# Padding two groups of SBUF tiles in a fused attention and token/channel mixer to multiples of 256 bytes

## The chip, the cores and the metric

The kernel runs on one core of one Trainium2 chip. The metric is the device time of one execution in microseconds. Three runs of the kernel before gave 799.47, 801.26 and 802.11 us; their median, 801.26 us, is the time that the change is measured against. All matrix work is in fp32 or in fp32r, a form of fp32 that TensorE takes in one pass; where full precision is wanted an fp32 value is held as a high and a low fp32r part.

## The reference, cut to what matters

```python
# B, H, S, D = 8, 8, 576, 64; attention inside chunks of 64 positions
scores = q_c @ k_c.T / sqrt(D);  attn = softmax(scores)
x = (attn @ v_c) as (B, S, 512)
h  = relu(x.T @ w_tok1) @ w_tok2          # tokens: 576 -> 256 -> 576
u  = x + h.T
h2 = relu(u @ w_ch1) @ w_ch2              # channels: 512 -> 1536 -> 512
return u + h2
```

## The kernel before, in words

All weights stay in SBUF as a high and a low part (tiles `kept_*`; for the channel matrices 24 tiles of 4096 bytes in each partition, made one after another from raw words while batch 0 is computed). A product of two split operands is three matmuls, `THREE`: high weight by high data, low weight by high data, high weight by low data. On TensorE the `kept_c` slice of 128 columns is the stationary operand (the "weights", loaded by LDWEIGHTS while the matmul before it streams) and the data tile is the moving operand of 512, 448 or 288 columns.

The work falls into three stages.

1. **The start** (about the first 54 us): nine attention tiles' loads, weight conversion, five attention tiles of batch 0, whose `v` tiles have 65 columns a head (a column of ones gives the row sums) and are allocated with `VPAD` columns, and batch 0's token mixing. Its result, split in high and low parts for two halves of 288 positions and four groups of 128 channels, is the one tile `both`.
2. **Batch 0's channel mixing** (to about 152 us): `ch1` (L584) and `ch2` (L626) run over 12 slices `f` with the pieces of `both`, or the hidden tiles `gh`, `gl`, as moving operands of 288 columns. Beside it ACT and DVE convert the rest of the weights and attention of batch 1 runs.
3. **Eight blocks of 512 positions** (the last one 448), here numbered 0 to 7, to the end. In each, for each of 12 slices `f`: 12 matmuls at L584 (four channel groups by `THREE`; moving operands `uh`, twice each, and `ul`, once each, four tiles of both), ACT and DVE write the hidden slice as `gh` and `gl`, and 12 matmuls at L626 (moving operands `gh` eight times, `gl` four times). At some `f` an attention step (L325 and L337, 64 small matmuls in the trace) is put in between. At the end of a block stand the token matmuls of a later batch (L491, L562).

TensorE's order is written by hand; DMAs are all issued from SP's queue in program order; ACT, DVE and POOL are ordered by a planner, which also places every SBUF tile at an address, for the time that it lives.

**Where the tiles lie.** In the program of the kernel before, the planner stacked the tiles by size. At the bottom lies `both` (address 1152, 18432 bytes a partition), above it `g1` (19584), the first weights, `xt` and `kept_t2`; from 68736 to 183424 a stack of 28 slots of 4096 bytes (the kept channel weights and `qk`); above it three slots of 2176 bytes for `v` tiles of the start (183424, 185600, 187776); and from 189952 to 228864 a stack of 19 slots of 2048 bytes. Tiles of 2048 bytes (`gh`, `gl`, `uh`, `ul`, `xh`, `xl`, `rh`, `rl` and others) lie in that upper stack, and also below, wherever a larger tile has died. Taken modulo 256, every data tile of 512 bytes or more below 183424 starts at 128 (with one exception, a `ul` of the last block); 2176 is 128 more than a multiple of 256; and every slot of 2048 bytes from 189952 up starts at 0. The channel weights all start at 128. Thus a moving operand "agrees" with its weights modulo 256 if it starts at 128. The tiles at the places that the prediction speaks of:

| groups of 12 matmuls | moving operands' addresses | of 12, agreeing |
|---|---|---|
| L584, block 0 | uh 194048 212480 218624 226816, ul 185600 198144 202240 214528 | 0 |
| L584, block 1 | uh 28800 51328 57472 183424, ul 33408 187776 208384 220672 | 10 |
| L584, block 2 | uh 43136 45184 47232 214528, ul 30848 35456 202240 226816 | 8 |
| L584, block 3 | uh 51328 55424 183424 212480, ul 21632 33408 53376 216576 | 9 |
| L584, block 4 | uh 30848 43136 45184 194048, ul 35456 196096 202240 218624 | 7 |
| L584, block 5 | uh 26240 55424 57472 212480, ul 51328 208384 210432 216576 | 7 |
| L584, block 6 | uh 1152 41600 177280 181376, ul 3200 35456 53376 179328 | 12 |
| L626, most slices | gh 222720 or, at every other slice, 37504; gl 224768 or 206336 | 0 or 8 |
| L626, block 6 at 675.8 us | gh and gl both at multiples of 256 | 0 |
| L626, block 6 at 681.4 us | gh at 128, gl at 0 | 8 |
| L626, block 6 at 692.4 us | gh 222720, gl 17536 | 4 |
| L626, block 6 at 697.8 us | gh 39552, gl 7296 | 12 |

In block 7, of 448 columns, the L626 groups at 745.4 and 760.1 us have 12 agreeing, the L584 groups 9, other L626 groups 0 or 8. The pieces of `both` are 1152 bytes apart, so every other one agrees.

Of the kernel before, what the change touches and what calls it, by code (L numbers as in the profile page):

```python
# [13 lines left out]
F32R = mybir.dt.float32r  # L14
# [4 lines left out]
P = 128  # L19
B, H, S, D = 8, 8, 576, 64  # L20
CH = 64
BK = 32
# [3 lines left out]
NDT = DM // P  # L26
# [3 lines left out]
HALF = S // 2  # L30
# [1 line left out]
QK = 2 * NHP * P  # L32
DV = D + 1
VW = 2 * NHP * DV
VPAD = -(-VW // BK) * BK
REBIAS = 2.0 ** -112
MOST = float.fromhex("0x1.dffcp-96")
THREE = ((0, 0), (1, 0), (0, 1))
# [28 lines left out]
def attention_mixer_kernel(ctx, tc, qk_in, vo_in, v_in, w1_in, w2_in, wc1_in, wc2_in, out):  # L67
# [22 lines left out]
    pool = ctx.enter_context(tc.tile_pool(name="pool", bufs=2))  # L90
# [39 lines left out]
    for key, src, lo, n in reversed(plan):  # L130
        name = "raw_" + "_".join(map(str, key))
# [128 lines left out]
    def load_v(i):  # L260
        if i < NTILE:
            v = pool.tile([P, VPAD], F32, tag="v1" if i > 4 else "v0", name="v", bufs=2 if i > 4 else 5)
            v = v[:, :VW].rearrange("p (a b c) -> p a b c", a=2, c=DV)
# [427 lines left out]
    r = [pool.tile([P, DM], F32, tag="gr", name="r", bufs=8) for _ in range(NT1)]  # L691
    nc.scalar.activation(out=r[0], in_=sums[0], func=AF.Relu)
    nc.vector.tensor_scalar_max(out=r[1], in0=sums[1], scalar1=0.0)
    both = pool.tile([P, 2, 2, NDT, HALF], F32R, tag="both", name="both", bufs=1)
    us = [[[both[:, n, w, m] for m in range(NDT)] for w in range(2)] for n in range(2)]
    low = None
    for m in range(NDT):
        convert(END_FILL[2 + m])
# [204 lines left out]
```

## Time and profile before

| | before |
|---|---|
| median of 3 runs | 801.26 us (799.47 to 802.11) |
| profiled execution, its own time | 799.71 us |
| span of the profiled execution | 797.9 us |
| TensorE busy | 783.7 us (98%) |
| weight loads (beside the matmuls) | 653.6 us (82%) |
| VectorE / ScalarE / GpSimd busy | 348.7 / 237.7 / 108.1 us |
| mean granted TensorE clock | 0.993 |

The page's first part gives busy time by engine, its fourth the chain of work that ended last. A matmul's record is longer than its turn, because the next one starts before it has drained; what a matmul costs in a row of matmuls is therefore read from start to start, or from the length of a merged piece of the chain divided by its count.

### The profile page before, as it was taken

The page shows a single profiled execution, that of the slowest core. Times are in us where ns is not written, and L with a number is a line of the kernel's source. Part 1 is how long each engine was busy: PE and PEld are TensorE (multiplying, and loading weights), DVE is VectorE, ACT ScalarE, POOL GpSimd, SP SyncE. Part 2 cuts the span into 40 slices and gives each one's busy share as a digit, 9 for nine tenths or more (in the row PEclk, how much of TensorE's full clock was granted, in tenths as well). Part 3 has the DMA queues.
Part 4 walks back from the last instruction along what each step waited for, and adds up shares of the span by engine and source line. Part 5 has one row for each costly group of instructions (what it writes and reads, how often), then busy time and mean ns, then how long its engine had stood idle before and what let it go on. Part 6 is the DMA issues. An engine that isn't in the chain of part 4 may idle for free.

```text
span 797.9 us, 14108 instructions
## 1 busy us (share of the span) xinstructions
PE 783.7 (98%) x5857; PEld 653.6 (82%) x5857; DVE 348.7 (44%) x627; ACT 237.7 (30%) x418; POOL 108.1 (14%) x94
## 2 busy tenths in 40 slices
PE   7899999999999999999999999999999999999998
PEld 4589998887888888888888788888887788888997
DVE  5788756644344442543444334535343314114112
ACT  6899733322231221222322222222312211111110
POOL 0000011310012010401041004100130104003300
PEclk7999999999999999999999999999999999999999
DMA  9935334344413540343323430435134201000101
GB/s 355 407 118 201 129 95 136 100 139 138 146 32 123 162 133 14 118 162 132 113 67 126 143 97 37 161 129 160 37 115 131 80 1 53 0 1 14 40 0 47
DMA packets 66415, 87.60 MB, mean 110 GB/s; under 512 B 7792, under 2 KB 41328, under 8 KB 66352
## 3 DMA queue, kind: packets, MB, share of 16 engines
q1 hardware_dynamic: 66352, 86.71, 32.3%
q8 instruction: 46, 0.75, 0.4%
q14 instruction: 17, 0.14, 0.1%
HBM read 59.81 MB, written 25.95 MB: 107 GB/s over the span
## 4 chain that ended last, share of the span: by engine, by line
PE 87%; DVE 4%; DMA 4%; ACT 3%; issue 1%; SPq 1%; DVEq 0%; ACTq 0%
PE acc L626 35%; PE ps_c L584 33%; PE ps_t L562 6%; PE ps_t L491 6%; PE ps_sv L325 2%; DMA raw_c<-in_wc 2%; PE ps_sv L337 2%; PE ps_t L534 1%; DMA v<-in_vo 1%; ACT low L174 1%; PE ps_t L528 1%; ACT wtop L164 1%; DVE wtop L184 1%; DVE o L634 1%; SPq L359 1%
## 5 line engine op out<-in xcount | busy, mean ns | idle before, releaser
L626 PE MATMUL acc<-gh,kept_c 128*128 128x512 f32 (+2 forms) x960 | 275.4, 375 | 1.2 <-ACT gh L606 0.7
L584 PE MATMUL ps_c<-uh,kept_c 128*128 128x512 f32 (+1 forms) x768 | 236.8, 389 | 0.0
L596 DVE SCALAR_TENSOR_TENSOR gl<-ps_c,gh 128x512 fp32r<-128x512 f32 (+2 forms) x108 | 70.9, 656 | 322.6 <-ACT gh L595 322.6
L626 PEld LDWEIGHTS acc<-gh,kept_c 128*128 128x128 f32 x960 | 170.8, 188 | 32.1 <-ACT gh L606 1.2
L626 PE MATMUL acc<-gl,kept_c 128*128 128x512 f32 (+2 forms) x480 | 172.2, 372 | 0.0
L584 PEld LDWEIGHTS ps_c<-uh,kept_c 128*128 128x128 f32 x768 | 144.1, 188 | 30.7
L595 ACT ACTIVATE gh<-ps_c 128x512 fp32r<-128x512 f32 (+2 forms) x108 | 61.6, 570 | 298.2 <-PE ps_c L584 298.2
L584 PE MATMUL ps_c<-ul,kept_c 128*128 128x512 f32 (+1 forms) x384 | 149.5, 389 | 0.1
L626 PEld LDWEIGHTS acc<-gl,kept_c 128*128 128x128 f32 x480 | 88.1, 188 | 15.5
L434 POOL TENSOR_TENSOR xl<-x,xh 128x512 fp32r<-128x512 f32 x28 | 36.7, 1312 | 362.4 <-ACT xh L433 318.1
L584 PEld LDWEIGHTS ps_c<-ul,kept_c 128*128 128x128 f32 x384 | 72.1, 188 | 15.6 <-DVE ul L574 0.5
L574 POOL TENSOR_TENSOR ul<-u,uh 128x512 fp32r<-128x512 f32 (+1 forms) x16 | 20.8, 1305 | 259.1 <-ACT uh L573 247.2
L562 PE MATMUL ps_t<-kept_t,rh 128*128 128x448 f32 (+7 forms) x224 | 48.5, 311 | 0.0
L584 PE MATMUL ps_c<-both,kept_c 128*128 128x288 f32 x288 | 45.1, 302 | 0.1
L376 ACT COPY pt<-pf 128x512 f32<-128x512 f32 x31 | 19.2, 620 | 80.1 <-DMA pf<-far 80.1
L305 ACT ACTIVATE pr<-pr 128x512 f32<-128x512 f32 x36 | 22.7, 629 | 63.2 <-DVE pr L301 63.2
L584 PEld LDWEIGHTS ps_c<-both,kept_c 128*128 128x128 f32 x288 | 40.1, 188 | 1.3 <-DVE gl L596 0.2
L562 PEld LDWEIGHTS ps_t<-kept_t,rh 128*128 128x128 f32 x224 | 37.5, 189 | 1.7
L636 POOL TENSOR_TENSOR o<-o,ul 128x512 f32<-128x512 f32 x28 | 38.5, 1406 | 1.5 <-DVE o L634 1.5
L568 DVE TENSOR_TENSOR u<-ps_t,xt 128x512 f32<-128x512 f32 (+1 forms) x32 | 21.8, 681 | 35.1 <-PE ps_t L562 33.2
L573 ACT CAST uh<-u 128x512 fp32r<-128x512 f32 (+1 forms) x32 | 19.5, 614 | 53.0 <-DVE u L568 53.0
L491 PE MATMUL ps_t<-xh,kept_t 128*128 128x512 f32 x112 | 34.9, 393 | 0.0
(87 smaller groups left out, 703.2 us busy)
## 6 DMA issues: line engine op xcount, KB each, us to landing
qk<-in_qk SPq DMA_DIRECT2D x36, 512.0 KB, 3.9
far<-blocks SPq DMA_DIRECT2D x63, 256.0 KB, 2.1
raw_c<-in_wc SPq DMA_DIRECT2D x24, 512.0 KB, 9.1
pf<-far SPq DMA_DIRECT2D x124, 64.0 KB, 1.9
out<-o SPq DMA_DIRECT2D x28, 256.0 KB, 2.0
v<-in_v SPq DMA_DIRECT2D x27, 256.0 KB, 4.1
xt<-far SPq DMA_DIRECT2D x100, 64.0 KB, 1.9
v<-in_vo SPq DMA_DIRECT2D x9, 260.0 KB, 8.0
```

The lines of the kernel that those rows point to most:

```text
L305: nc.scalar.activation(out=pr, in_=pr, func=AF.Exp, scale=1.0 / float(D) ** 0.5)
L434: nc.gpsimd.tensor_tensor(out=xl, in0=t["x"], in1=xh.bitcast(F32), op=ALU.subtract)
L491: nc.tensor.matmul(ps, lhsT=lhsT, rhs=rhs, start=(n == 0 and q == 0), stop=(n == len(mt) - 1 and q == len(terms) - 1),)
L562: nc.tensor.matmul(ps[:, at:at + n], lhsT=lhsT[:, cols], rhs=rhs, start=(q == 0), stop=(q == len(terms) - 1),)
L568: nc.vector.tensor_tensor(out=u.rearrange("p (i c) -> p i c", c=BK), in0=ps[:, :width].rearrange("p (i c) -> p i c", c=BK), in1=block_x(k) ...
L573: nc.scalar.copy(out=uh[m], in_=u)
L574: (nc.vector if m in UL_ON_VECTOR else nc.gpsimd).tensor_tensor(out=ul[m], in0=u, in1=uh[m].bitcast(F32), op=ALU.subtract)
L584: nc.tensor.matmul(ps[:, :width], lhsT=weights["c1", f][:, wi, k * P:(k + 1) * P], rhs=u[ui][k], start=(k == 0 and q == 0), stop=(k == NDT ...
L595: nc.scalar.activation(out=gh, in_=ps[:, :width], func=AF.Relu)
L596: nc.vector.scalar_tensor_tensor(out=gl, in0=ps[:, :width], scalar=0.0, in1=gh.bitcast(F32), op0=ALU.max, op1=ALU.subtract)
L626: nc.tensor.matmul(accs[e], lhsT=weights["c2", f][:, wi, e * P:(e + 1) * P], rhs=g[gi], start=(f == 0 and q == 0), stop=(f == NFC - 1 and ...
L636: nc.gpsimd.tensor_tensor(out=o, in0=o, in1=u[1][e].bitcast(F32), op=ALU.add)
```

## The change

`VPAD`, the allocated width of the 65-column `v` tiles, is rounded up to 256 elements instead of 32: the tile takes 640 columns (2560 bytes) in place of 544 (2176 bytes). The last dimension of `both` grows from 288 to 320 columns (1280 bytes in place of 1152; the tile takes 20480 bytes), of which the first 288 are used. What is loaded, computed and written is the same, and so is the order in which it is written down.

```diff
-VPAD = -(-VW // BK) * BK
+VPAD = -(-VW // (8 * BK)) * 8 * BK
...
-    both = pool.tile([P, 2, 2, NDT, HALF], F32R, tag="both", name="both", bufs=1)
-    us = [[[both[:, n, w, m] for m in range(NDT)] for w in range(2)] for n in range(2)]
+    both = pool.tile([P, 2, 2, NDT, HALF + BK], F32R, tag="both", name="both", bufs=1)
+    us = [[[both[:, n, w, m, :HALF] for m in range(NDT)] for w in range(2)] for n in range(2)]
```

## Rows read from the trace of the kernel before

**Rows 1.** The page, parts 1 and 4: busy time by engine; the chain by engine.
```profile
PE 783.7 (98%) x5857; PEld 653.6 (82%) x5857; DVE 348.7 (44%) x627; ACT 237.7 (30%) x418; POOL 108.1 (14%) x94
PE 87%; DVE 4%; DMA 4%; ACT 3%; issue 1%; SPq 1%; DVEq 0%; ACTq 0%
```
**Rows 2.** Busy time by stretch: PE, weight loads, DVE, ACT, POOL, clock, DMA, GB/s.
```profile
0.00:54.00 54.00, 45.61 (x491) 31.42 (x492) 38.82 (x87) 42.17 (x75) 0.91 (x10) 0.91 0.85 325
54.00:152.00 98.00, 95.85 (x888) 89.82 (x888) 69.70 (x137) 59.89 (x119) 10.69 (x10) 1.00 0.39 125
...
570.00:660.00 90.00, 90.00 (x627) 74.35 (x626) 31.80 (x52) 18.22 (x30) 14.49 (x11) 1.00 0.22 72
660.00:735.00 75.00, 75.00 (x338) 62.41 (x337) 18.50 (x28) 10.70 (x19) 9.69 (x8) 1.00 0.04 15
```
**Rows 3.** Groups by line and shape: busy us, mean ns | idle before.
```profile
L626 PE MATMUL acc<-gh,kept_c 128*128 128x512 f32 x672 | 212.7, 397 | 0.0
L584 PE MATMUL ps_c<-uh,kept_c 128*128 128x512 f32 x672 | 209.5, 393 | 0.0
...
L626 PE MATMUL acc<-gl,kept_c 128*128 128x512 f32 x336 | 132.3, 394 | 0.0
L584 PE MATMUL ps_c<-ul,kept_c 128*128 128x512 f32 x336 | 132.0, 393 | 0.1
```
**Rows 4.** Chain in order of time, block 6 (no attention): start us, us, what.
```profile
675.83 2.79 PE acc L626 x12
...
681.36 2.75 PE acc L626 x12
684.10 2.72 PE ps_c L584 x12
...
692.35 2.75 PE acc L626 x12
...
697.84 2.72 PE acc L626 x12
```
**Rows 5.** The same, first two slices of L584 in blocks 1 to 6.
```profile
239.70 5.47 PE ps_c L584 x24
...
324.69 5.55 PE ps_c L584 x24
...
410.44 5.51 PE ps_c L584 x24
...
494.26 5.56 PE ps_c L584 x24
...
579.90 5.57 PE ps_c L584 x24
...
664.92 5.44 PE ps_c L584 x24
```
**Rows 6.** The same, blocks 0 and 1, with attention steps.
```profile
177.16 2.79 PE acc L626 x12
179.95 2.80 PE ps_c L584 x12
...
183.84 2.98 PE acc L626 x12
...
247.96 2.76 PE ps_c L584 x12
```
**Rows 7.** The same, block 7 of 448 columns.
```profile
742.97 2.43 PE ps_c L584 x12
745.40 2.47 PE acc L626 x12
...
750.31 2.45 PE acc L626 x12
```
**Rows 8.** The same, token matmuls at the end of block 5.
```profile
646.00 6.51 PE ps_t L491 x28
```
**Rows 9.** The chain from 60 to 112 us, shares by line.
```profile
by line: ACT low L174 11.5%; DMA raw_c<-in_wc 9.1%; DVE wtop L184 8.5%; ACT wtop L164 8.4%; issue 8.4%; DMA far<-blocks 7.7%; SPq L359 7.0%; DVE kept_c L231 6.8%; ACT low L165 4.4%; DVE wtop L178 4.2%; DVE blocks L348 3.1%; ACT kept_c L225 
```
**Rows 10.** Waits, whole span, then PE's from 152 us: us, times, longest us.
```profile
ACT pt L376 <- DMA pf<-far: 80.1, 30, 5.2
...
PEld ps_c L584 <- DVE ul L574: 0.5, 1, 0.5
```
**Rows 11.** DMA issues: count, KB each, median us from issue to landing.
```profile
v<-in_vo SPq DMA_DIRECT2D x9, 260.0 KB, 8.0
```

## The prediction, made before the change was run

> **What bounds the kernel now.** I read the page first: TensorE is busy for 98% of the span and carries 87% of the chain that ended last [rows 1]. Then the stretches: in the first 54 us ACT, DVE and DMA are as full as PE; from 54 to 152 us PE stands still for 2 of 98 us with DVE at 70 of them; from 570 to 660 us, one block with attention, PE is busy for all of it, the others for a third or less, and from 660 to 735 us, where there is no attention, it is the same with almost no DMA [rows 2]. So from 152 us on the kernel is a row of matmuls, and what a matmul takes from start to start is the time. The groups of 512 columns are 672 + 672 with high parts and 336 + 336 with low parts, 2016 matmuls in 168 groups of 12 [rows 3].
>
> The chain in order of time has these groups as pieces. In block 6, without attention, a piece of L626 takes 2.79, 2.75 or 2.72 us, with the same shapes and the same lines [rows 4]. What differs is where the moving operands lie, which the table of places gives: 2.79 with none of the 12 agreeing with the weights modulo 256, 2.75 with 8 and also with 4, 2.72 with 12. L584 shows the same over the blocks: a block's first two slices, 24 matmuls, take 5.44 us with 12 of 12 agreeing, 5.47 with 10, 5.51 with 9, 5.55 with 8, 5.56 and 5.57 with 7 [rows 5], and 2.80 for 12 with none [rows 6]. That is one order without an exception, over tiles in many places. I take it that a matmul whose moving operand lies 128 off from the weights being loaded beside it takes some 6 ns longer: (2.79 - 2.72) / 12.
>
> **The change, part by part.**
>
> *The v tiles.* No instruction is added or removed. The nine loads bring 260 KB each as before [rows 11]; the added columns are neither loaded nor read, so the start pays nothing for them, and the same holds for `both`. What changes is the stack of tiles: if the planner stacks by size as now, `both` and the 4096-byte tiles end at 183424 + 2048 = 185472, three slots of 2560 bytes end at 193152, and both are 128 modulo 256. The upper stack then starts at 128 instead of 0, and every `gh`, `gl`, `uh`, `ul`, `xh` and `xl` agrees with its weights wherever it lies. The order of the matmuls is written by hand, so only places and the waits for a place can change.
>
> What this is worth, by blocks 0 to 6. L584 goes to 2.72 a group: from 2.80 in block 0 [rows 6], and from half of the 24-matmul pieces in the others [rows 5]: 2.735 (later 2.76 [rows 6], which I take), 2.775, 2.755, 2.78, 2.785, 2.72. The gains are 0.08 + 0.04 + 0.055 + 0.035 + 0.06 + 0.065 + 0 = 0.335 us a slice, times 12 slices: 4.0 us. L626 goes from 2.79 or 2.75 to 2.72 [rows 4]; beside attention a group with 8 agreeing takes 2.79 as well [rows 6]. I take 72 groups of blocks 0 to 5 at a gain of 0.07, less about ten that run at 2.75 now and gain 0.03: 4.6 us; block 6 alternates, 12 groups at 0.04: 0.5 us. Together 9.1 us.
>
> The groups right after an attention step take 2.98 [rows 6], 0.19 more than their neighbours. The trace has none of these with 12 agreeing. Their extra may stay (I take that: the small matmuls before them have other operands) or go too, five to a block in six blocks, 30 x 0.1 = 3 us more at most if half of it goes; or the attention may take the gain away, which is a rival below.
>
> The token matmuls, L491: 28 in 6.51 us, 232 ns each [rows 8], against 2.72 / 12 = 227. Seven such pieces, 196 matmuls, about 1 us if all agree; some do now, so 0.8.
>
> The last block, 448 columns: here it is the other way round. The fully agreeing group takes 2.47 us, a group of 9 agreeing 2.43, one with none 2.45 [rows 7]. 24 groups at about +0.025 are 0.6 us lost.
>
> *The pieces of* `both`. They move to a spacing of 1280 bytes, so all agree instead of every other one. They are used in batch 0's stage alone. There the chain runs through conversions on ACT and DVE, DMAs and SP's queue, and no PE line has a place among the first dozen [rows 9]: a few ns a matmul are covered by waits for those. If that cover were gone the gain is at most the 2 us that PE now stands still for plus what the matmuls shrink; I take 0, and 0.5 us either way for the range.
>
> *Memory.* The upper stack has room for 17 slots of 2048 bytes instead of 19, (228864 - 193152) / 2048 = 17.4. The 4096-byte stack moves up by the 2048 bytes of `both`, and since `both` dies at about 152 us, one slot more is free below from then on. I take no new wait: in the main stage PE's longest wait for another engine is 0.5 us, once [rows 10].
>
> Sum: 4.0 + 5.1 + 0.8 - 0.6 = 9.3 us faster. Against its own execution, 799.7 us with a span of 797.9, that is 790.4; the median is 1.55 us above that execution, so 801.3 - 9.3 = 792.0 us.
>
> **The rivals.**
>
> *Attention keeps the groups late.* In block 1 the same L584 tiles take 2.735 a group at the block's start and 2.76 right after a slow L626 group [rows 5, 6]; and with 8 agreeing L626 takes 2.75 in block 6 but 2.79 in block 0 [rows 4, 6]. A group that starts late stays late. If each attention step sets that lateness afresh and agreement doesn't cure it, groups in blocks 0 to 5 settle near 2.76 in place of 2.72: 144 x 0.04 = 5.8 us of the gain are gone, and it comes to 801.3 - 3.5 = 797.8 us. Against it: in block 6 a 2.72 follows directly on a 2.75 [rows 4].
>
> *The planner doesn't stack as now.* It places tiles by their lives, and a sliver of 128 bytes or another count of `v` slots leaves some at 0. With half of the tiles agreeing about half is left: 796.7 us.
>
> *The places are not the cause.* The tiles at 0 are nearly all those of the upper stack, so the difference could come with the region, or with what runs when those tiles are in use. Then nothing changes: 801.3 us. Against it: 183424 and 187776 count as agreeing in blocks 1 and 3 and fit the order [rows 5], and in block 6 neighbours with one load differ [rows 4].
> [...]
>
> *Slower: a place comes free later.* With two slots fewer in the upper stack, the `pf` tile of an attention step (the transposed probabilities, fetched by DMA for ACT's copy at L376) may get a slot whose last reader ends later. SP's queue is in order, so the fetch and all loads behind it wait, ACT's copy is late, and TensorE stands at L337, since its order is fixed. ACT waits for that DMA in 30 steps already, 80.1 us in all [rows 10], covered by the matmuls of a slice or more. If the cover is used up, 31 steps at the 0.5 us of the longest PE wait [rows 10] cost 15.5 us: 801.3 - 9.3 + 15.5 = 807.5 us. It decides from (9.3 + 2.4) / 31 = 0.38 us a step. The third of idle time on the other engines [rows 2] speaks against it.
>
> **How the numbers follow.** About 0.3%, 2.4 us, is what a measurement of this kernel can tell from no change, so faster means under 798.9 us, slower over 803.7. Forecast 792.0 us: 0.65. Attention keeps groups late, 797.8: 0.13, of which 0.09 is under 798.9. Half the tiles, 796.7: 0.08, of which 0.06 under. No cause, 801.3: 0.07. Slower, 807.5: 0.07. Faster 0.65 + 0.09 + 0.06 = 0.80; same 0.04 + 0.02 + 0.07 = 0.13; slower 0.07. The range goes down to 788.5 (the 3 us after attention steps and 0.5 for batch 0) and up to 799.5, which takes in the first two rivals with the spread of 1.5 us between runs, and leaves out 0.07 + 0.07 and some ends.
>
> **What would show it.** In the changed profile the 24-matmul pieces of L584 should be 5.44 in every block, L626's pieces 2.72 in block 6 without alternation, the L491 piece 6.35, the block 7 pieces 2.47, and the stage up to 152 us as long as now. L584 pieces at 2.76 beside attention show the first rival; a mix of 2.72 and 2.79 the second; unchanged pieces with all places at 128 the third; new idle time of PE ahead of L337 the last. The prediction fails if agreement isn't what makes 2.79 into 2.72.

## The result, and the profile after

The changed kernel takes 792.83 us, median of 4 runs (791.87 to 794.42); the kernel before takes 800.51 us, median of 4 (799.47 to 802.11). The ratio is 0.9904, 95% interval 0.9879 to 0.9929: 7.7 us faster, and clear of no change. The forecast was 792.0 us, 9.3 us faster. The profiled executions took 799.71 us before and 792.71 us after.

One statement ahead of the prediction is wrong. The new `VPAD` rounds 520 columns up to a multiple of 256, which is 768 columns, 3072 bytes, and not 640 columns, 2560 bytes. The upper stack thus starts at 194688, not at the prediction's 193152, and is smaller than I worked out. 3072 is a multiple of 256 as well, so the places modulo 256 came out as forecast: every fp32r weight tile and moving operand starts at 128, and all 2209 matmuls of 512 columns agree with the weights loaded beside them, where 1086 did before. What 2560 bytes would have done is one of the experiments.

The page of the changed kernel, busy time by engine and the chain by engine:

```profile
PE 774.0 (98%) x5857; PEld 652.1 (82%) x5857; DVE 349.3 (44%) x627; ACT 237.9 (30%) x418; POOL 108.2 (14%) x94
PE 86%; DMA 5%; ACT 4%; DVE 3%; SPq 1%; issue 1%; DVEq 0%; ACTq 0%
```

TensorE lost 9.7 us of busy time and stays the bound [against rows 1]; the other engines do what they did. The chain in order of time, block 6 of the changed kernel (start us, us, what):

```profile
658.43 5.44 PE ps_c L584 x24
663.87 2.72 PE acc L626 x12
666.59 2.72 PE ps_c L584 x12
669.31 2.72 PE acc L626 x12
672.03 2.72 PE ps_c L584 x12
674.75 2.72 PE acc L626 x12
```

The alternation of 2.79, 2.75 and 2.72 [rows 4] is gone; every piece of 12 in this block is 2.72, and the first one, of 24, is twice that. The first two slices of the other blocks, from the same view, which took 5.47 to 5.57 us before [rows 5]:

```profile
239.33 5.44 PE ps_c L584 x24
...
323.21 5.44 PE ps_c L584 x24
...
407.87 5.44 PE ps_c L584 x24
...
490.56 5.44 PE ps_c L584 x24
...
575.00 5.44 PE ps_c L584 x24
```

Block 1 with its attention step, the token matmuls at the end of block 5, and block 7:

```profile
244.77 2.72 PE acc L626 x12
247.49 2.72 PE ps_c L584 x12
250.21 0.62 PE ps_sv L325 x32
250.83 0.47 PE ps_sv L337 x32
251.30 2.95 PE acc L626 x12
254.25 2.72 PE ps_c L584 x12
...
639.66 6.35 PE ps_t L491 x28
...
735.90 2.44 PE ps_c L584 x12
738.33 2.43 PE acc L626 x12
```

Beside attention too L584 is at 2.72 now, where it was 2.80 and 2.76 [rows 6]. The group right behind an attention step went from 2.98 only to 2.95. L491 went from 6.51 [rows 8] to 6.35, as 28 x 227 ns asks. Block 7 is at 2.43 to 2.44 throughout.

Where the time went, summed from the starts of successive matmuls in the two traces (after minus before, us; each matmul counted up to the start of the next):

```
stage                    L584    L626    L491    other   all
up to block 0           -0.28   +0.07   -0.08   +0.75   +0.46
block 0                 -0.91   -0.57   +0.65   -0.01   -0.84
blocks 1 to 6           -3.21   -3.17   -0.65   +0.37   -6.66
block 7 (448 columns)   -0.11   -0.20    0       0      -0.31
span                                                    -7.36
```

### The profile page after: what moved, and what is told of

It is laid out like the page before. It is cut to its first block, busy times and chain, and to the rows that moved or that the text cites. A ratio compares the mean times of both kernels' runs of the same rounds, so it can differ in the third digit from the quotient of the medians.

```text
span 790.6 us, 14145 instructions
## 1 busy us (share of the span) xinstructions
PE 774.0 (98%) x5857; PEld 652.1 (82%) x5857; DVE 349.3 (44%) x627; ACT 237.9 (30%) x418; POOL 108.2 (14%) x94
## 4 chain that ended last, share of the span: by engine, by line
PE 86%; DMA 5%; ACT 4%; DVE 3%; SPq 1%; issue 1%; DVEq 0%; ACTq 0%
PE acc L626 34%; PE ps_c L584 33%; PE ps_t L562 6%; PE ps_t L491 5%; DMA raw_c<-in_wc 2%; PE ps_sv L325 2%; PE ps_sv L337 2%; PE ps_t L534 1%; DMA v<-in_vo 1%; DMA far<-blocks 1%; ACT low L165 1%; PE ps_t L528 1%; SPq L359 1%; ACT low L174 1%; ACT wtop L164 1%
## 5 line engine op out<-in xcount | busy, mean ns | idle before, releaser
L626 PE MATMUL acc<-gh,kept_c 128*128 128x512 f32 (+2 forms) x960 | 272.8, 372 | 1.7 <-ACT gh L595 1.0
L584 PE MATMUL ps_c<-uh,kept_c 128*128 128x512 f32 (+1 forms) x768 | 234.1, 386 | 0.0
L626 PEld LDWEIGHTS acc<-gh,kept_c 128*128 128x128 f32 x960 | 170.5, 188 | 30.9 <-ACT gh L595 1.5
L626 PE MATMUL acc<-gl,kept_c 128*128 128x512 f32 (+2 forms) x480 | 170.7, 369 | 0.0
L584 PEld LDWEIGHTS ps_c<-uh,kept_c 128*128 128x128 f32 x768 | 144.1, 188 | 27.5
L584 PE MATMUL ps_c<-ul,kept_c 128*128 128x512 f32 (+1 forms) x384 | 148.3, 386 | 0.0
L626 PEld LDWEIGHTS acc<-gl,kept_c 128*128 128x128 f32 x480 | 88.0, 188 | 14.3
L584 PEld LDWEIGHTS ps_c<-ul,kept_c 128*128 128x128 f32 x384 | 72.1, 188 | 14.3 <-DVE ul L574 0.4
L574 POOL TENSOR_TENSOR ul<-u,uh 128x512 fp32r<-128x512 f32 (+1 forms) x16 | 20.9, 1307 | 256.3 <-ACT uh L573 219.3
L376 ACT COPY pt<-pf 128x512 f32<-128x512 f32 x31 | 19.2, 620 | 91.1 <-DMA pf<-far 91.1
L584 PE MATMUL ps_c<-both,kept_c 128*128 128x288 f32 x288 | 44.8, 302 | 0.2
L584 PEld LDWEIGHTS ps_c<-both,kept_c 128*128 128x128 f32 x288 | 39.7, 188 | 1.5 <-ACT g L592 0.4
L562 PE MATMUL ps_t<-kept_t,rl 128*128 128x448 f32 (+7 forms) x112 | 34.8, 311 | 0.0
```

Source lines behind the costliest of these rows:

```text
L562: nc.tensor.matmul(ps[:, at:at + n], lhsT=lhsT[:, cols], rhs=rhs, start=(q == 0), stop=(q == len(terms) - 1),)
L574: (nc.vector if m in UL_ON_VECTOR else nc.gpsimd).tensor_tensor(out=ul[m], in0=u, in1=uh[m].bitcast(F32), op=ALU.subtract)
L584: nc.tensor.matmul(ps[:, :width], lhsT=weights["c1", f][:, wi, k * P:(k + 1) * P], rhs=u[ui][k], start=(k == 0 and q == 0), stop=(k == NDT ...
L626: nc.tensor.matmul(accs[e], lhsT=weights["c2", f][:, wi, e * P:(e + 1) * P], rhs=g[gi], start=(f == 0 and q == 0), stop=(f == NFC - 1 and ...
```

## The experiments

All ten are variants of the changed kernel or of a part of it. In each the time of the kernel before is from the same chip. Where a run gives a tile another size, the planner also puts other tiles into other slots; what is compared is the places modulo 256, and the pieces of the chain in block 6 tell a matmul's price from a wait.

**Which of the two parts.** First the `v` tiles alone:

```diff
-    both = pool.tile([P, 2, 2, NDT, HALF + BK], F32R, tag="both", name="both", bufs=1)
+    both = pool.tile([P, 2, 2, NDT, HALF], F32R, tag="both", name="both", bufs=1)
```

> The v tiles alone are padded (768 columns, 3072 bytes); both stays as in the kernel before. All 2209 matmuls of 512 columns then agree with the weights loaded beside them modulo 256, 137 of 555 of 288 columns do not. Theory (agreement of the long matmuls from 152 us on is what pays): the time of the changed kernel, 792.8 us, within 1 us; plain groups of 12 at 2.72 us. Rival (the pieces of both matter for the time): half a microsecond to 2 us slower, 793.5 to 795 us, with the stage from 54 to 152 us longer.

Measured 793.79 us (792.62 to 794.35) against 800.64, ratio 0.9906 (0.9892 to 0.9921). That is the whole gain, within the spread of the runs. In its trace the groups of 12 with the pieces of `both`, half of which agree, take 1.60 us against 1.58 in the changed kernel, where all agree, so a short matmul gains from agreement too. Block 0 begins at 151.8 us all the same, against 152.3 in the changed kernel and 151.8 in the kernel before: nothing of that gain is seen in the stage's length, which fits the chain of before [rows 9].

This trace also has a wait that the changed kernel has not. In block 2 TensorE stands ahead of L337 for ACT's copy of `pt`, whose fetch landed late:

```profile
PE ps_sv L337 <- ACT pt L376: 1.6, 1, 1.6
```

That is the sign by which the prediction's last rival was to be known. More of it below.

Then `both` alone:

```diff
-VPAD = -(-VW // (8 * BK)) * 8 * BK
+VPAD = -(-VW // BK) * BK
```

> The tile both alone is padded; the v tiles keep 2176 bytes. The stack lies 2048 bytes higher as in the changed kernel, but its upper part starts at 0 modulo 256 again: 1269 of 2209 matmuls of 512 columns are 128 off. Theory: no gain, 800.5 to 801.5 us, groups between 2.72 and 2.80 us as before. Rival (the moved stack or the pieces of both bring the gain): 792.8 to 797 us.

Measured 800.61 us against 800.64, ratio 1.000 (0.9990 to 1.0009): nothing. The rival that the moved stack brings the gain falls.

**Agreement, or the new arrangement.** The same slots, with those above the three `v` slots 3 x 128 bytes further, which is 128 modulo 256:

```diff
+VPAD = 800
```

> The changed kernel with v tiles of 3200 bytes in place of 3072: every tile lies in the same slot as in the changed kernel, but those above the three v slots are 128 bytes further, and 1045 of 2209 matmuls of 512 columns are 128 off. Theory: the gain is gone, 799 to 801 us, and the groups show 2.79 to 2.80 where no operand agrees. Rival (the new arrangement of slots and its waits bring the gain, not agreement): 792.8 us, groups at 2.72.

Measured 800.64 us against 800.64, ratio 1.0001 (0.9991 to 1.0011). 128 bytes a `v` tile, with nearly every tile in the slot that it has in the changed kernel, take the gain away (a few tiles lie elsewhere). Block 6 of this kernel, the chain in order of time:

```profile
668.55 2.73 PE acc L626 x12
671.29 2.77 PE ps_c L584 x12
674.05 2.79 PE acc L626 x12
676.84 2.77 PE ps_c L584 x12
679.62 2.72 PE acc L626 x12
682.34 2.77 PE ps_c L584 x12
```

At 674.05 none of the 12 agrees, at 679.62 all do, in the same block with the same load: the alternation is back. This is the control that the prediction lacked, since in the kernel before agreeing and lying low in memory went together.

**The place, or the difference.** Everything 128 bytes higher, weights included:

```diff
-... dynamic_dma_scratch_size=1024)
+... dynamic_dma_scratch_size=1152)
```

> The changed kernel with everything in SBUF 128 bytes higher (the reserved area at the bottom is 1152 bytes in place of 1024): weights and moving operands all start at 0 modulo 256 instead of at 128. Theory (only the difference counts): 792.8 us within 1 us, groups at 2.72. Rival (a moving operand is fast at 128 modulo 256, slow at 0, whatever the weights' place): all groups at 2.79 or more, 803 us or more.

Measured 794.09 us (792.05 to 796.42), ratio 0.9913 (0.9889 to 0.9937): the median is 1.3 us over the changed kernel's, a little outside the 1 us expected, but the intervals of the two ratios overlap. The groups are at 2.72 throughout block 6:

```profile
667.58 2.72 PE acc L626 x12
670.30 2.72 PE ps_c L584 x12
```

Moving operands that start at 0 are fast when the weights start at 0. So it is the difference of the two addresses that counts. The profiled execution, the slowest of the four, has three single stalls of 1.5, 0.9 and 0.9 us against the changed kernel. Its waits name what came late: at the start of block 0 the tiles `ul`, written by POOL and DVE at L574, and twice ahead of L337 ACT's copy of `pt` (L376, 0.8 us each).

**How close must they be.** The tiles above the `v` slots at other distances:

```diff
+VPAD = 784      # then 792
```

> The changed kernel with v tiles of 3136 bytes: the slots are those of the changed kernel, but the tiles above the three v slots lie 192 bytes further, so that of 2209 matmuls of 512 columns 1158 agree, 539 are 192 off and 506 are 64 off. Theory A (only equality modulo 256 is fast): 799 to 801 us, as with 128 off. Theory B (the loss grows with the distance, 64 being half of 128): about 796.5 us. Theory C (equality modulo 64 is enough): 792.8 us, plain groups at 2.72.

Measured 800.33 us against 801.06, ratio 0.9991 (0.9982 to 1.0000).

> The same with v tiles of 3168 bytes: tiles above the v slots lie 32 bytes past agreement, those beside them 96; 1158 matmuls of 512 columns agree, 539 are 32 off, 488 are 96 off. Theory A: 799 to 801 us. Theory B: 794 to 796 us. Theory C (modulo 64): slower than with 192 and 64 off, 799 to 801 us against 792.8 us there.

Measured 801.99 us against 801.06, ratio 1.0009 (1.0000 to 1.0018). That is 1 us slower than Theory A's range, and nearest to it: being 32 bytes off costs as much as 128, so a loss that grows with the distance is out, and so is equality modulo 64, since 192 bytes off is slow. In the traces, the mean time from start to start of a 512-column matmul where it and the three before it are equally far from the weights loaded beside them:

```
bytes past agreement      0      32     64     96     128    192
ns, 512 columns         227.0  233.5  229.1  233.7  232.5  233.3
```

(0 is from the changed kernel, 128 from the kernels before, with `both` alone and with 3200 bytes, the others from these two.) At 64 bytes past agreement the loss is about a third; why it is less there than at 192 is open, and to that extent Theory A isn't the whole either. That equality modulo 256 is enough, and not modulo 512, the changed kernel's matmuls of 288 columns show: 132 of them lie 256 off modulo 512 and take 131 ns in the median, as those with no difference do (of 512 columns there are only eight such, at 227 ns). Block 6 of the second of these kernels shows the price in the chain:

```profile
666.43 5.57 PE ps_c L584 x24
672.00 2.75 PE acc L626 x12
674.75 2.80 PE ps_c L584 x12
677.54 2.80 PE acc L626 x12
```

**The size of the pad.** 2560 bytes:

```diff
+VPAD = 640
```

> The changed kernel with v tiles of 640 columns, 2560 bytes, in place of 768 columns, 3072 bytes. All 2209 matmuls of 512 columns agree. Theory (agreement counts, not the size of the pad): 792.8 us within 1 us, plain groups at 2.72. Rival (the larger pad with its other slots matters): another time by 2 us or more.

Measured 793.53 us (792.15 to 794.78), ratio 0.9901 (0.9882 to 0.9920), with groups of 2.72 in block 6. My slip in the size made no difference that these runs can tell; 512 bytes less a tile do the same.

**Which weights.** The low part of each channel weight 128 bytes off:

```diff
-        parts = ... = kept.tile([P, 2, n], F32R, name=name)
+        parts = ... = kept.tile([P, 2, n + BK * (key[0][0] == "c")], F32R, name=name)[:, :, :n]
```

> The changed kernel with 32 unused columns behind each of the two parts of a channel weight: the high part stays at 128 modulo 256, the low part starts at 0; all moving operands stay at 128. In a group of three (high weight, low weight, high weight with the low data) the low weight is loaded while the first matmul streams, and is the second one's own. If what counts is the weights loaded beside a matmul: the first of three is the slow one, the second is not. If a matmul's own weights count: the second is. Either way a third of the matmuls is off, as in the groups of the kernel before with 8 of 12 agreeing: 2.745 to 2.75 us a plain group, 168 x 0.025 to 0.03 = 4 to 5 us, about 797 us. Rival (moving operands' places alone count): 792.8 us.

Measured 800.16 us against 801.06, ratio 0.9986 (0.9977 to 0.9996). No moving operand changed its place modulo 256, so the rival that their places alone count is out. But the loss against the changed kernel is about 7 us (7.3 by the medians, 6.9 by the spans of the profiled executions), not 4 to 5. Its chain in block 6:

```profile
669.74 2.77 PE acc L626 x12
672.51 2.77 PE ps_c L584 x12
675.29 2.77 PE acc L626 x12
678.06 2.77 PE ps_c L584 x12
```

Each group loses 0.05 us; the two lines together lose 7.5 us in its trace. From start to start the three matmuls of a triple take 232.5, 234.1 and 226.7 ns: the first, beside which the low weights are loaded, and also the second, whose own weights they are. I had expected one of the two. The next run asks for the own weights by themselves, at L626 only:

```diff
+        parts = ... = kept.tile([P, 2, n + BK * (key[0] == "c2")], F32R, name=name)[:, :, :n]
...
+        return gh, pool.tile([P, N + 2 * BK], F32R, tag="gl", name="gl")[:, BK:BK + width]
...
-            for q, (wi, gi) in enumerate(THREE):
+            for q, (wi, gi) in enumerate(((0, 0), (0, 1), (1, 0))):
```

> The changed kernel with, at L626 alone, the low weights 128 bytes off (at 0 modulo 256), the low data gl at 0 too, gh and the high weights at 128, and the order high weight by gh, high weight by gl, low weight by gh. Each matmul's moving operand then agrees with the weights that are loaded while it streams (those of the next matmul), but the second and the third of three do not agree with their own weights, which were loaded before. If only the weights loaded beside a matmul count: 792.8 us, L626 at 2.72. If its own weights count as well (in the run with low weights off, two of three matmuls were slow, 233, 234 and 227 ns, though one of three was off by the weights loaded beside it): L626 at 2.77, 84 x 0.053 = 4.5 us, 797.3 us.

Measured 798.95 us against 800.93, ratio 0.9980 (0.9970 to 0.9989), where 797.3 was expected if the own weights count. The chain in block 6:

```profile
669.24 2.76 PE acc L627 x12
672.00 2.74 PE ps_c L584 x12
674.74 2.76 PE acc L627 x12
677.50 2.74 PE ps_c L584 x12
```

The line of `ch2` is L627 here. Every matmul agrees with the weights loaded beside it, and yet the groups take 2.76, and the L584 groups behind them, all agreeing, 2.74. So agreement with the next weights alone wasn't enough here: with some own weights off the groups lost 0.04 us each. Of the 6.1 us over the changed kernel the trace puts 3.6 behind the start of block 0 and 2.6 ahead of it, where block 0 begins at 154.9 us instead of 152.3; what makes that part is open. The nanoseconds of single matmuls in these groups run from 224 to 236 without a simple order, so which matmul of three pays, and how much, stays open. So does whether two loads of weights one after the other at different places modulo 256, which this run and the one before it also have, cost something by themselves.

**The full price.** All of L626 off, and all of L584 and L491 agreeing:

```diff
-        return [pool.tile([P, N], F32R, tag=tag, name=tag)[:, :width] for tag in ("gh", "gl")]
+        return [pool.tile([P, N + 2 * BK], F32R, tag=tag, name=tag)[:, BK:BK + width] for tag in ("gh", "gl")]
```

> The changed kernel with gh and gl both 128 bytes off, so that all matmuls of L626 disagree and all of L584 and L491 agree. Theory (each of 12 loses 6 ns): L626 from 2.72 to 2.79, 84 x 0.07 = 5.9 us, 798.7 us, L584's plain groups at 2.72. Rival (a group's own part and a lasting lateness of what follows): L584 groups right after a slow L626 are slow as well, 2.735 or more, and the time is 800 us or more.

Measured 798.59 us (797.30 to 800.13), ratio 0.9968 (0.9954 to 0.9982): 5.8 us over the changed kernel by the medians, 5.1 by the ratios, where 84 x 0.07 = 5.9 was expected. The chain in block 6, with `ch2` at L628:

```profile
668.76 2.79 PE acc L628 x12
671.55 2.73 PE ps_c L584 x12
674.29 2.79 PE acc L628 x12
677.08 2.73 PE ps_c L584 x12
```

Plain groups are as forecast, 2.79 against 2.72, and the loss stays with the groups that are off, but for 0.01 us of the next one. That the total is near 5.9 us is partly luck. From start to start the 84 groups of L626 lose 4.8 us against the changed kernel, not 5.9, because the 27 behind an attention step lose only 0.03 us each (2.86 to 2.89). L584 loses 1.9 us, 0.9 of it in one late group at the start of block 0, which has a wait for `ul`.

## Why the prediction was right, and where its steps were not

**The bound and the cause: right.** The kernel from 152 us on is a row of matmuls (TensorE was busy for 642.24 of 645 us there), and agreement of the moving operand with the weights sets the price of a 512-column matmul: 227 ns or 232 to 233. The prediction spoke only of the weights being loaded beside a matmul; in the runs with the low weights off and with the pairs, groups took 2.77 and 2.76 us with own weights off, where the weights beside them alone would have made 2.75 and 2.72. The own weights, or two loads at different places one after the other, count too; those runs don't part the two. Nor do 6 ns for each matmul that is off add up in mixed groups: five of 12 off would make 2.75 us, and L584 took 2.78 in blocks 4 and 5 [rows 5]. The forecast went by the measured lengths of the groups and did not hang on that sum. The runs with 128 bytes more above the `v` tiles (no gain), with all addresses moved (full gain) and with L626 alone off (5.8 us) show it as a cause. The rival that places do not matter falls.

**The places: right, with a wrong number.** The planner stacked as forecast; only the `v` slot is 3072 bytes.

**L584: right in size.** 4.0 us forecast; 0.91 + 3.21 = 4.12 measured over blocks 0 to 6.

**L626: mis-sized.** 5.1 us forecast, 0.57 + 3.17 = 3.74 measured. The step that failed is the gain of 0.07 for 72 groups, in which I counted those behind an attention step like the others. These, 27 in the traces (I had said 30), went from 2.98 or 2.97 to 2.95, a gain of 0.03: 27 x 0.04 = 1.1 us missing, most of the difference. The last experiment shows the same from the other side. The extra behind an attention step isn't a matter of agreement: in the changed kernel, with all operands agreeing, it is still 0.23 us, where it was 0.19.

**L491: right where nothing else stood in the way.** 0.8 us forecast; blocks 1 to 6 give 0.65, but block 0 lost as much again. The chain there, in the kernel before and then in the changed kernel:

```profile
220.11 6.48 PE ps_t L491 x28
```

```profile
212.20 4.63 DMA far<-blocks
...
219.21 2.40 DMA xc<-x
221.61 0.01 issue
221.62 0.70 DVE stack L450
222.31 0.04 issue
222.36 3.94 PE ps_t L491 x16
```

In the kernel before the 28 matmuls ran through. Now they stop after 12 of 28 for the tile `stack`. Before, its first half was ready at about 221.7 us and its first matmul started at 222.72, so there was 1.0 us to spare. In the changed kernel TensorE comes to L491 0.9 us earlier (219.01 in place of 219.95), and `stack` is ready 0.6 us later, because the fetch `xc` behind it was issued at 218.70 in place of 218.16. So the faster matmuls took most of the slack, and the fetch the rest.

Such waits come with the gain. The one at L491 is there in the five kernels whose L584 groups run at 2.72 or 2.73 us (the changed one, `v` alone, all addresses moved, 2560 bytes, and L626 alone off), where L491 in block 0 takes 0.3 to 0.8 us more than in the run with the pairs, and not in the rest. The one ahead of L337, by which the prediction's last rival was to be known, is not in the changed kernel, but it stands once at 1.6 us in the run with the `v` tiles alone, twice at 0.8 us with all addresses moved, and once at 0.8 us with 2560 bytes; in the kernels that keep the old time TensorE doesn't wait there. The lines for the changed kernel, all addresses moved and 2560 bytes, in this order:

```profile
PE ps_t L491 <- DVE stack L450: 0.5, 1, 0.5
...
PE ps_sv L337 <- ACT pt L376: 1.6, 2, 0.8
...
PE ps_sv L337 <- ACT pt L376: 0.8, 1, 0.8
```

So that rival's mechanism exists; it costs 0.8 to 1.6 us in a profiled execution that has it, not 15.5. The argument against it was also misread: rows 2 show the other engines busy for about a third of the time, not idle for a third.

**Block 7: wrong in sign.** I forecast +0.6 us, because the two fully agreeing groups took 2.47 [rows 7]; it became 0.31 us shorter, with all groups at 2.43 to 2.44. With L626 alone off they take 2.44 to 2.45 there, so at 448 columns agreement is worth about 1 ns a matmul. The two groups of before stood between others that were off, so two pieces of 12 were no measure of what a row of agreeing groups does. The same mistake in the other direction would have been to take the mean difference between all agreeing and all other matmuls of the kernel before, some 2 ns, as the gain, instead of the whole pieces.

**The first rival, attention keeps groups late: fell.** The L584 group after the group behind an attention step is at 2.72 in every block: a late group no longer slows the next one. That fits the next operands' being off again in the kernel before, but how the lateness was passed on there was not shown.

**The stage up to 152 us.** Forecast 0 with 0.5 either way, measured +0.46, and the runs with one part each begin block 0 at 151.8 and 151.4; over all runs but the one with the pairs it is 151.1 to 152.9. No effect can be told from that spread.

Together: of 9.3 us forecast the profiled executions show 7.0 (7.4 in their spans) and the medians 7.7. In the spans 1.4 are missing at L626, 0.8 at L491 and 0.5 at the start; block 7 gave 0.9 more than forecast and L584 0.1; the 0.35 that is left lies in the other lines. That the time came within 0.8 us of the forecast is in part luck: misses both ways, and a median of the kernel before that came out 0.75 us lower with the fourth run.

## What to carry to other kernels

When TensorE is the bound, group its pieces on the chain by where their operands lie, not only by line and shape: pieces of one shape and different length, here 2.72 to 2.80 us, are the sign. A size that is not a multiple of 256 bytes, in a tile that has nothing to do with the row of matmuls, can put everything stacked above it out of step: with 3200 bytes in place of 3072 for each `v` tile this kernel took 800.64 us, against 792.83. So pad the odd tile instead of moving the many. Read a price from long stretches in which all operands are in one state; in the kernel before a mixed neighbourhood hid more than half of it (some 2 ns a matmul showed, of 5.5), and a lone good group in it looked bad (2.47 us in block 7 [rows 7], where a row of such groups takes 2.43 to 2.44). And when the bound engine gets faster, look again at what fed it just in time: the attention steps' fetches, for which TensorE did not wait before, took 0.8 to 1.6 us of the gain in the profiled executions of the kernels that waited there.

## What the runs showed of the hardware

An fp32r matmul leaves one record of TensorE in the trace (2016 for the 168 groups of 12 [rows 3]), a plain fp32 one two (20 at L500 for ten matmuls). The records of 512 columns are 393 to 397 ns long [rows 3], longer than the step from start to start.

An fp32r matmul of 512 columns (granted clock 1.00 [rows 2]) takes 227 ns from start to start if its moving operand's start address, that of its weights and that of the weights loaded beside it are equal modulo 256 bytes, and 232 to 234 ns if the moving operand is 32, 96, 128 or 192 bytes off, 229 if it is 64 off. With 288 columns the groups of 12 took 1.58 us with all 12 agreeing, against 1.60 with half of them; with 448 the difference is about 1 ns a matmul. The pieces of block 6, where DMA is at 4% and the other engines are busy for a quarter of the time or less [rows 2], show the price as clearly as those beside attention; that the other engines have no part in it was not tested by itself. That groups take 2.76 with the weights beside them agreeing and some of the own weights off I had not expected; what in the hardware makes these differences was not shown.
